# Keeping the sines and cosines of E and the activation hf in PSUM, with two phase buffers and three banks for the gated unit

## The chip, the core and the metric

The kernel runs on one core of one Trainium2 chip. Five engines work side by side there: TensorE (PE, with its weight loads shown apart as PEld), VectorE (DVE), ScalarE (ACT), GpSimd (POOL) and SyncE (SP), the last of which only issues transfers here. Each engine carries out its own list of instructions in order, and instructions on different engines wait for each other through semaphores. TensorE writes its results to PSUM, which this kernel uses as eight banks of 128 partitions by 512 fp32 values; VectorE and ScalarE read and write both PSUM and the large on-chip memory SBUF, and GpSimd works on SBUF alone in this kernel. The metric is the device time of one launch in microseconds (us).

## The reference, cut to what matters

The input `x` has 2048 tokens of 448 channels. After a layer norm the result is the sum of the input, a state-space convolution and a gated unit:

```python
def _A_ref(u, log_A_real, A_imag, C_real, C_imag, log_dt, D_skip):
    L = u.shape[1]
    dt = jnp.exp(log_dt)
    A = -jnp.exp(log_A_real) + 1j * A_imag
    C = (C_real + 1j * C_imag) * dt[:, None]
    pos = jnp.arange(L)
    P = jnp.exp((A * dt[:, None])[:, :, None] * pos[None, None, :])
    K = 2.0 * jnp.einsum("dn,dnl->dl", C, P).real
    ...                                  # y = causal convolution of u with K, by FFT of length 2L
    return y + u * D_skip[None, None, :]

def _B_ref(x, w_gate, w_up, w_down):
    g = jnp.einsum("bsd,df->bsf", x, w_gate)
    u = jnp.einsum("bsd,df->bsf", x, w_up)
    return jnp.einsum("bsf,fd->bsd", _sigmoid(g) * u, w_down)

xn = _layernorm(x)
return x + _A_ref(xn, ...) + _B_ref(xn, ...)
```

There are 448 channels with 256 complex modes each in the convolution, and 1792 hidden columns in the gated unit. All is fp32.

## The kernel before, in words

Two Python generators write the program: `conv()` for the convolution and `glu()` for the gated unit. Each yields after a piece of work with a weight, and the loop at the end of `s4d_glu_kernel` always continues the one whose share of its planned total is smaller, so that pieces of both alternate in the program. A scheduler then sets the order of the instructions on each engine from a simulated timeline: the earlier instruction in the program has precedence, `hp(HP)` lifts instructions ahead of it by 300 places, and `tc.issue_after(ins)` keeps instructions behind another of the same engine. On the chip that order is fixed.

**The convolution** has four stages. The first (to about 130 us of the span) normalises the input, turns it for the gated unit (`x_transpose`), takes the first step of its Fourier transform (`x_spec`, through the PSUM tile `tr`) and prepares the modes' rates, phases and weights (`prep`, `turn`), mostly on VectorE. The second, `kgen` (139 to 541 us), builds the convolution's kernel. Its 56 chunks (`cn`) hold 8 channels each. The exponential of a mode at a position is a product of a factor E, at 64 fine positions, and a factor F, at 32 coarse positions. For each chunk `ahead(cn)` makes the phases of E and F with two matmuls into `tr` (two banks, one buffer), and ScalarE turns them into sines and cosines in the SBUF tile `S` (L547 to L550; two tiles `S0` and `S1` take turns). GpSimd multiplies up the magnitudes `me` and `mf` for two chunks at a time (`magnitudes`, L505 and L517), with two squarings on ScalarE (L530). VectorE multiplies magnitudes with sines and cosines: L604 and L605 make `Et`, L606 makes `Ft`. TensorE sums over the modes, 64 small matmuls a chunk into `ko` (L620). Every four chunks `first_stage` takes a Fourier step of the finished part, through two PSUM tiles `kp` and `kq`, copied to SBUF at L571. `ahead(cn + 1)` stands before the products of `cn` in the program. The third and fourth stages (`spectra`, from about 541 us) multiply the spectra and go back to time.

**The gated unit** goes through two halves of the tokens, and in each through groups of two or three blocks of 128 hidden columns. A step, `gate()`, is one block for 512 tokens: 11 matmuls make the gate's PSUM tile and 11 more the up tile (L712, each operand being split into a high and a low part), ScalarE takes a tanh of the gate into `th` (L720), VectorE makes `hf = (th + 1) * up` (L723), ScalarE rounds it to `hh` (L728), and VectorE takes the rest `hl = hf - hh` (L730). `hf`, `hh` and `hl` are SBUF tiles before the change, so that the bank of the up tile is free once L723 has read it. After a group come eight tiles `po` of the down projection (L826), each added to the accumulator by VectorE at L831. Towards the end of the first half `pair_first` and `pair_turn` bring in the rest of the tokens, through four and two PSUM tiles.

**PSUM before:** the pool `psg` has one tag `gu` with four banks, which the gate and up tiles, `po`, `kq` and the tiles of `pair_first` and `pair_turn` share. The pool `psk` of the first two stages has the other four: `tr` with two, `ko` and `kp` with one each. A tile is given a bank that is free, and its first writer waits for the last reader of the tile that held the bank.

## Time and profile before

| | |
|---|---|
| median of three runs | 728.39 us (727.42 to 731.0) |
| span of the profiled execution, first to last instruction | 723.7 us |
| the profiled execution's own time | not given apart from its span |
| mean granted TensorE clock over the span | 0.983 |
| busy: PE, DVE, ACT, POOL | 676.0, 567.5, 420.8, 380.5 us |
| HBM traffic | 158 GB/s over the span |

The profile comes from one execution. Its span leaves out what lies before the first and after the last instruction; against the median that is 728.39 - 723.7 = 4.7 us. Busy time is the time in which an engine has an instruction under way; matmuls are pipelined, so a busy PE may still wait a little between two of them. A row of a group gives the line, the engine, the operation, the tiles written and read, the shapes, the count, the busy time together and the mean of one in ns, and then the idle time of the engine just before them, with what ended it.

### The profile page before, as it was taken

How to read it: one execution, taken by the hardware profiler on the slowest of the kernel's cores; microseconds unless marked ns; L12 is line 12 of the kernel's file. 1: busy time of each engine (PE TensorE's matmuls, PEld its weight loads, DVE VectorE, ACT ScalarE, POOL GpSimd, SP SyncE). 2: the span in 40 equal slices, each digit the busy share in tenths (PEclk: the TensorE clock that was granted, in tenths of full speed). 3: DMA queues.
4: the chain of work that ended last, by engine and by line, in shares of the span. 5: the costliest groups of instructions: out<-in, count | busy, mean ns of one | idle time of the engine just before them, and what ended most of it. 6: DMA issues, size and time to landing. Idle time of an engine off the chain costs nothing.

```text
span 723.7 us, 19120 instructions
## 1 busy us (share of the span) xinstructions
PE 676.0 (93%) x7789; PEld 532.0 (74%) x7789; DVE 567.5 (78%) x778; ACT 420.8 (58%) x650; POOL 380.5 (53%) x425
## 2 busy tenths in 40 slices
PE   2898799997998999998999999999999999999996
PEld 1675688786876788565777887888877777767785
DVE  5799997699999999999589988987874555655544
ACT  3645455678677778899387777866742222322320
POOL 2120028699888778879646874785864000451002
PEclk9998899999999999999999999999999999999999
DMA  9946328534414445354753242232169999999745
GB/s 204 224 119 186 97 81 251 173 97 167 162 52 135 160 149 173 93 196 141 242 166 120 70 141 87 98 107 72 47 163 247 279 256 218 246 258 244 178 135 163
DMA packets 92711, 115.72 MB, mean 160 GB/s; under 512 B 12432, under 2 KB 81040, under 8 KB 92368
## 3 DMA queue, kind: packets, MB, share of 16 engines
q1 hardware_dynamic: 83040, 93.92, 47.4%
q10 hardware_dynamic: 7040, 14.91, 6.5%
q0 software_dynamic: 2544, 5.67, 3.2%
q8 instruction: 61, 1.00, 0.6%
q14 instruction: 26, 0.21, 0.1%
HBM read 69.70 MB, written 44.76 MB: 158 GB/s over the span
## 4 chain that ended last, share of the span: by engine, by line
PE 69%; DVE 13%; DMA 6%; ACT 5%; issue 3%; SPq 1%; POOL 1%; ACTq 0%; DVEq 0%; POOLq 0%
PE gu L712 28%; PE po L826 16%; PE sp L912 7%; PE ko L620 6%; PE pv L939 4%; PE tr L539 4%; DVE Ft L606 2%; DVE Et L604 2%; DVE Et L605 2%; DMA acc_d<-acc 1%; DVE hl L730 1%; DMA xe<-in_A_u_dram 1%; PE pv L976 1%; PE kp L565 1%; DVE m L321 1%
## 5 line engine op out<-in xcount | busy, mean ns | idle before, releaser
L517 POOL TENSOR_TENSOR me<-me,pm 128x32 f32<-128x32 f32 (+1 forms) x168 | 145.7, 867 | 85.0 <-DVE Et L605 72.9
L517 POOL TENSOR_TENSOR mf<-mf,pm 128x64 f32<-128x64 f32 (+1 forms) x112 | 120.7, 1078 | 4.9
L712 PE MATMUL gu<-xh,wh 128*128 128x512 f32 x336 | 100.3, 404 | 3.2 <-ACT xh L220 3.2
L712 PE MATMUL gu<-xh,wl 128*128 128x512 f32 x336 | 95.9, 393 | 0.0
L712 PE MATMUL gu<-xl,wh 128*128 128x512 f32 x336 | 95.1, 390 | 0.0
L826 PE MATMUL po<-dh,hh 128*128 128x448 f32 (+1 forms) x227 | 86.4, 380 | 6.1 <-DVE acc L831 2.5
L604 DVE TENSOR_TENSOR Et<-me,S 128x1024 f32<-128x1024 f32 x56 | 82.3, 1470 | 8.8 <-ACT S L550 4.5
L605 DVE TENSOR_TENSOR Et<-me,S 128x1024 f32<-128x1024 f32 x56 | 79.0, 1411 | 8.5 <-ACT me L530 7.6
L606 DVE TENSOR_TENSOR Ft<-mf,S 128x1024 f32<-128x1024 f32 x56 | 79.9, 1426 | 6.8 <-ACT S L550 4.4
L826 PE MATMUL po<-dl,hh 128*128 128x448 f32 (+1 forms) x227 | 84.2, 371 | 0.0
L826 PE MATMUL po<-dh,hl 128*128 128x448 f32 (+1 forms) x227 | 83.5, 369 | 0.0
L547 ACT ACTIVATE S<-tr 128x1024 f32<-128x1024 f32 x56 | 57.8, 1032 | 41.0 <-PE tr L539 33.4
L712 PEld LDWEIGHTS gu<-xh,wh 128*128 128x128 f32 x336 | 61.3, 190 | 22.3 <-ACT xh L220 4.6
L728 ACT CAST hh<-hf 128x512 fp32r<-128x512 f32 x56 | 35.0, 625 | 71.1 <-DVE hf L723 59.8
L712 PEld LDWEIGHTS gu<-xh,wl 128*128 128x128 f32 x336 | 63.3, 189 | 15.0 <-DVE pl L313 0.7
L620 PEld LDWEIGHTS ko<-Et,Ft 128*32 128x32 f32 x3584 | 53.5, 110 | 27.4 <-issue 17.1
L712 PEld LDWEIGHTS gu<-xl,wh 128*128 128x128 f32 x336 | 63.0, 188 | 14.0 <-issue 0.7
L620 PE MATMUL ko<-Et,Ft 128*32 128x64 f32 x3584 | 63.6, 222 | 9.2 <-DVE Ft L606 4.7
L723 DVE SCALAR_TENSOR_TENSOR hf<-th,gu 128x512 f32<-128x512 f32 x56 | 38.1, 680 | 37.4 <-PE gu L712 27.7
L550 ACT ACTIVATE S<-S,hpi 128x1024 f32<-128x1024 f32 x56 | 65.5, 1170 | 0.0
L831 DVE SCALAR_TENSOR_TENSOR acc<-po,acc 128x448 f32<-128x448 f32 (+1 forms) x81 | 48.7, 610 | 19.4 <-PE po L826 19.3
L730 DVE TENSOR_TENSOR hl<-hf,hh 128x512 fp32r<-128x512 f32 x56 | 51.2, 914 | 12.6 <-ACT hh L728 12.6
(199 smaller groups left out, 1288.6 us busy)
## 6 DMA issues: line engine op xcount, KB each, us to landing
sk_d<-sk ACTq DMA_DIRECT2D x14, 512.0 KB
sx<-x_d SPq DMA_DIRECT2D x32, 224.0 KB
skl<-sk_d SPq DMA_DIRECT2D x16, 448.0 KB
vp<-v_d SPq DMA_DIRECT2D x16, 448.0 KB
v_d<-vt SPq DMA_DIRECT2D x60, 112.0 KB
wt_d<-wh SPq DMA_DIRECT2D x9, 512.0 KB
wt_d<-wl SPq DMA_DIRECT2D x9, 512.0 KB
wl<-wt_d SPq DMA_DIRECT2D x9, 512.0 KB
```

The lines of the kernel that those rows point to most:

```text
L517: ins = nc.gpsimd.tensor_tensor(m[:, :, w + a : 2 * w : n], m[:, :, a:w:n], par(base + i).unsqueeze(2).to_broadcast([128, 4 * DC, w // n]) ...
L547: nc.scalar.activation(rows(cs), pv, AF.Abs)
L550: sins[:] = [nc.scalar.activation(cs, cs, AF.Sin, scale=-TWO_PI, bias=hpi)]
L604: v.tensor_tensor(Et[:, :, :, 32:64], two(me[:, :, 32:64]), S[:, 1::-1], ALU.mult)
L605: v.tensor_tensor(Et[:, :, :, 0:32], two(me[:, :, 0:32]), S[:, 1:3, :, ::-1], ALU.mult)
L606: fts[:] = [v.tensor_tensor(Ft, two(mf), S[:, 3:5], ALU.mult)]
L620: nc.tensor.matmul(ko[32 * j : 32 * j + 32, sl], Ft[:, cc, DC * h + 4 * q + j], Et[:, cc, DC * h + 4 * q + j], start=(k == 0), stop=(k == ...
L712: glu_mm[:] = [nc.tensor.matmul(ps, a_, b_, start=(n == 0), stop=(n == len(mm) - 1))]
L730: v.tensor_tensor(hl, hf, hh, ALU.subtract)
L826: glu_mm[:] = [nc.tensor.matmul(po[:, ds], a_[:, bs], w_[:, ds], start=(n == 0), stop=(n == 3 * fc - 1))]
L831: v.scalar_tensor_tensor(acc[:, b, ds], po[:, ds], 0.5, acc[:, b, ds], ALU.mult, ALU.add)
L912: mm = nc.tensor.matmul(to, tb[:kk, t, 64 * c : 64 * c + 64], rhs, start=True, stop=True, skip_group_check=True,)
```

## The change

The tile `tr` gets two buffers of two banks. Each of its two banks now holds one kind of phase, E's or F's, in place of half of the modes of both; so `ahead` needs four matmuls of 256 columns where it had two of 512, with each block of phases loaded as weights twice. ScalarE takes the absolute values of both into `S` (one instruction, as before), and then four instructions of 512 elements make the sine of F in `S`, the sine of E in its own place in PSUM, the cosine of E in the bank that held F's phases, and the cosine of F in `S`. The negated sine of E is no longer made. `S` shrinks from five parts to three.

VectorE reads the sines and cosines of E from PSUM. The product for the upper 32 positions stays one instruction of 1024 elements; that for the lower 32 becomes two of 512, the second of which (`scalar_tensor_tensor`) also changes the sign. The product for F reads `S` as before.

In `gate()`, `hf` is no longer a tile of its own: L723 writes it over the up tile in PSUM, and L728 and L730 read it there.

The tag `gu` has three banks instead of four. `ko` keeps its bank; the separate bank of `kp` is gone, and `kp` and `kq` both take banks of `gu`. `x_spec`, `turn` and the first `x_transpose` use the buffers of `tr`.

```diff
         if nb == 4:
-            two = psc[-1].tile([128, 2, 512], F32, name="tr", bufs=1)
-            banks = [two[:, 0], two[:, 1]] + [psc[-1].tile([128, 512], F32, name=n, bufs=1) for n in ("ko", "kp")]
+            two = [psc[-1].tile([128, 2, 512], F32, name="tr", bufs=2) for _ in range(2)]
+            banks = [t[:, i] for t in two for i in range(2)]
...
-                ps = psg.tile([128, 512], F32, name="gu", bufs=4)
+                ps = psg.tile([128, 512], F32, name="gu", bufs=3)
...
-            ("S1", [128, 5, 2 * DC, 32], F32), ("Et1", [128, 2, 2 * DC, 64], F32),
+            ("S1", [128, 3, 2 * DC, 32], F32), ("Et1", [128, 2, 2 * DC, 64], F32),
...
             S = tl[f"S{cn % 2}"]
-            ps = psc[-1].tile([128, 2, 512], F32, name="tr", bufs=1)
+            ps = psc[-1].tile([128, 2, 512], F32, name="tr", bufs=2)
             ph = pht[cn // 2 % 2]
             for h in range(2):
-                nc.tensor.matmul(
-                    ps[:, h], ph[:, cn % 2, 128 * h : 128 * h + 128], sel, start=True, stop=True
-                )
+                for c in range(2):
+                    x = slice(256 * c, 256 * c + 256)
+                    nc.tensor.matmul(
+                        ps[:, c, 256 * h : 256 * h + 256], ph[:, cn % 2, 128 * h : 128 * h + 128], sel[:, x],
+                        start=True, stop=True,
+                    )
...
-            nc.scalar.activation(rows(cs), pv, AF.Abs)
-            nc.scalar.activation(rows(S[:, 0:5:4]), pv, AF.Sin, scale=TWO_PI)
-            nc.scalar.activation(rows(S[:, 2:3]), pv[:, :, 0:1], AF.Sin, scale=-TWO_PI)
-            sins[:] = [nc.scalar.activation(cs, cs, AF.Sin, scale=-TWO_PI, bias=hpi)]
-            return S
+            ph_e, ph_f = ps[:, 0], ps[:, 1]
+            row = lambda i: S[:, i].rearrange("p m s -> p (m s)")
+            nc.scalar.activation(S[:, 0:2].rearrange("p c m s -> p c (m s)"), ps, AF.Abs)
+            nc.scalar.activation(row(2), ph_f, AF.Sin, scale=TWO_PI)
+            nc.scalar.activation(ph_e, ph_e, AF.Sin, scale=TWO_PI)
+            nc.scalar.activation(ph_f, row(0), AF.Sin, scale=-TWO_PI, bias=hpi)
+            sins[:] = [nc.scalar.activation(row(1), row(1), AF.Sin, scale=-TWO_PI, bias=hpi)]
+            return S, ps.rearrange("p c (m s) -> p c m s", s=32)
...
             pss = [
-                psc[-1].tile([128, 8, 2, 32], F32, name="kp", bufs=1),
-                psg.tile([128, 8, 2, 32], F32, name="kq", tag="gu", bufs=4),
+                psg.tile([128, 8, 2, 32], F32, name=n, tag="gu", bufs=3) for n in ("kp", "kq")
             ]
...
-                v.tensor_tensor(Et[:, :, :, 32:64], two(me[:, :, 32:64]), S[:, 1::-1], ALU.mult)
-                v.tensor_tensor(Et[:, :, :, 0:32], two(me[:, :, 0:32]), S[:, 1:3, :, ::-1], ALU.mult)
-                fts[:] = [v.tensor_tensor(Ft, two(mf), S[:, 3:5], ALU.mult)]
+                lo = me[:, :, 0:32]
+                v.tensor_tensor(Et[:, :, :, 32:64], two(me[:, :, 32:64]), ee[:, ::-1], ALU.mult)
+                v.tensor_tensor(Et[:, 0, :, 0:32], lo, ee[:, 1, :, ::-1], ALU.mult)
+                v.scalar_tensor_tensor(Et[:, 1, :, 0:32], ee[:, 0, :, ::-1], -1.0, lo, ALU.mult, ALU.mult)
+                fts[:] = [v.tensor_tensor(Ft, two(mf), S[:, 1:3], ALU.mult)]
...
-        hf = pg.tile([128, 512], F32, name="hf", bufs=1)
+        hf = pgu[1]
```

17 lines of the change are left out of this document (7 added, 10 removed).

## The prediction

> **What bounds the kernel now.** I read the page first: its span, the busy shares and the engines on the chain that ended last.
>
> ```profile
> span 723.7 us, 19120 instructions
> PE 676.0 (93%) x7789; PEld 532.0 (74%) x7789; DVE 567.5 (78%) x778; ACT 420.8 (58%) x650; POOL 380.5 (53%) x425
> PE 69%; DVE 13%; DMA 6%; ACT 5%; issue 3%; SPq 1%; POOL 1%; ACTq 0%; DVEq 0%; POOLq 0%
> ```
>
> TensorE is busy for 93% of the span and holds 69% of the chain. VectorE, whose work the change lightens, can therefore give back only time in which TensorE stands still. Where that is, the busy times by stage tell: one row each for the first and the second half of the building of the convolution's kernel, and for the spectra.
>
> ```profile
> core 0: us, PE busy (x) PEld busy (x) DVE busy (x) ACT busy (x) POOL busy (x), PEclk, DMA share, GB/s
> 140.00:350.00 210.00, 196.44 (x2877) 151.55 (x2876) 199.28 (x206) 167.93 (x253) 175.82 (x177) 0.98 0.43 136
> 350.00:545.00 195.00, 192.79 (x2982) 159.38 (x2981) 157.70 (x161) 137.27 (x197) 132.03 (x151) 1.00 0.39 121
> 545.00:723.70 178.70, 172.45 (x1405) 131.86 (x1403) 98.08 (x190) 44.74 (x85) 36.26 (x47) 1.00 0.90 222
> ```
>
> From 140 to 350 us VectorE is busy for 95% and TensorE idle for 210 - 196.4 = 13.6 us; the granted clock of 0.98 costs about 0.02 x 210 = 4.2 us more. From 350 to 545 TensorE is idle for 2.2 us with VectorE at 81%; after that VectorE is at 55% and no line of the change has much weight. So the prize lies between 140 and 350 us and is at most 13.6 + 4.2 = 17.8 us, with 2.2 behind it. Third, TensorE's own waits between 130 and 545 us (total, times, longest):
>
> ```profile
> PE ko L620 <- DVE Ft L606: 4.7, 7, 1.9
> PE ko L620 <- DVE Et L604: 4.6, 2, 2.9
> PE kp L565 <- ACT ks L633: 2.5, 3, 1.0
> PE po L826 <- DVE xr L224: 2.4, 2, 1.4
> ```
>
> Three of the four longest, 11.7 us, end with VectorE.
>
> **The products and hl on VectorE.** Durations (shortest, median, longest) of the two products for Et, of hf and of hl:
>
> ```profile
> L604 DVE TENSOR_TENSOR Et<-me,S x56: 1207/1328/2115, 139.2 to 531.3; 128x1024 f32<-128x1024 f32 x56
> L605 DVE TENSOR_TENSOR Et<-me,S x56: 1206/1224/2178, 140.3 to 532.5; 128x1024 f32<-128x1024 f32 x56
> L723 DVE SCALAR_TENSOR_TENSOR hf<-th,gu x56: 627/678/689, 27.9 to 691.8; 128x512 f32<-128x512 f32 x56
> L730 DVE TENSOR_TENSOR hl<-hf,hh x56: 618/691/2645, 30.3 to 693.2; 128x512 fp32r<-128x512 f32 x56
> L419 DVE TENSOR_TENSOR b<-b,m 112x512 f32<-112x512 f32 x2 | 1.4, 680 | 0.0
> ```
>
> L604, L605 and L730 read two SBUF tiles and vary by a factor of 1.8 to 4. L723 has the length of L730 but reads one operand in PSUM, and its 56 instances all lie within 627 to 689 ns, with GpSimd at work beside it for most of the time. I read this as a stretching by GpSimd that a PSUM operand avoids, and price the new instructions at the unstretched lengths: 1207 ns for the 1024 elements of L604, 680 ns for each of the two halves of L605 and for L730. L606 keeps two SBUF operands and its length. The busy time of L604, L605 and L730 in the two stages, in that order:
>
> ```profile
> 140.00:350.00 210.00, 41.46 (x30) 0.98 0.43 136
> 350.00:545.00 195.00, 39.98 (x26) 1.00 0.39 121
> 140.00:350.00 210.00, 44.54 (x30) 0.98 0.43 136
> 350.00:545.00 195.00, 34.46 (x26) 1.00 0.39 121
> 140.00:350.00 210.00, 17.18 (x16) 0.98 0.43 136
> 350.00:545.00 195.00, 16.65 (x18) 1.00 0.39 121
> ```
>
> From 140 to 350 us: L604 41.5 - 30 x 1.207 = 5.3; L605 44.5 - 60 x 0.68 = 3.7; L730 17.2 - 16 x 0.68 = 6.3; together 15.3 us off VectorE's 199.3, which falls to 88%. From 350 to 545 us: 8.6 - 0.9 + 4.4 = 12.1 us, off an engine that was no bound. What reaches TensorE: of the 11.7 us of waits I take 8, as the time won doesn't fall exactly where TensorE waited, and with fewer stops 3 of the 4.2 us of clock: **-11 us**. Bounds: 0, if the waits only move, and -20 (17.8 + 2.2).
>
> [...]
>
> **ScalarE.** The phases' four instructions before:
>
> ```profile
> L547 ACT ACTIVATE S<-tr x56: 1003/1028/1087, 135.1 to 527.8; 128x1024 f32<-128x1024 f32 x56
> L548 ACT ACTIVATE S<-tr x56: 1010/1022/1087, 136.0 to 528.8; 128x1024 f32<-128x1024 f32 x56
> L549 ACT ACTIVATE S<-tr x56: 596/605/667, 136.9 to 529.7; 128x512 f32<-128x512 f32 x56
> L550 ACT ACTIVATE S<-S,hpi x56: 1135/1165/1227, 137.9 to 530.1; 128x1024 f32<-128x1024 f32 x56
> ```
>
> Before 1.03 + 1.02 + 0.61 + 1.17 = 3.82 us. After: the absolute values 1.03, two sines of 512 at 0.61, two cosines with a bias at 1.17 - (1.03 - 0.61) = 0.74 each: 3.72 us. That saves 0.1 us a chunk on an engine at 80%, and E's products may start after four of the five, 0.83 us sooner. I count 0; it widens no wait. A write to PSUM by ScalarE has no row; if it cost as much as an SBUF write, nothing changes.
>
> **TensorE's phases.** Four matmuls of 256 columns instead of two of 512. The end of the trace has matmuls of 448 and 224 columns in a row, the first two rows two apart, the last two eight apart; then the weight load of a phase matmul:
>
> ```profile
> 716.32 0.37 PE L826 MATMUL po<-dh,hh 128*128 128x448 f32 x1
> 716.74 0.37 PE L826 MATMUL po<-dh,hl 128*128 128x448 f32 x1
> 716.94 0.27 PE L826 MATMUL po<-dh,hh 128*128 128x224 f32 x1
> 717.83 0.28 PE L826 MATMUL po<-dh,hl 128*128 128x224 f32 x1
> L539 PEld LDWEIGHTS tr<-sel,ph x112: 186/188/338, 132.0 to 527.2; 128*128 128x128 f32 x112
> ```
>
> Starts are 0.21 us apart at 448 columns and 0.111 us at 224, so about 0.0125 us + 0.44 ns a column: 0.125 us at 256 and 0.24 us at 512. Four against two: 0.50 - 0.48 = +0.02 us, and I take 0.04 us x 56 = **+2.2 us**, since all of it lies on the busy engine. Bounds: 0, and 2 x 0.188 x 56 = +21 us if the two added loads were in the open; in the row of 224 columns they are not. The new second buffer takes no wait in exchange: `tr` of chunk cn + 1 needs the Et products of cn - 1, which the 64 ko matmuls ahead of it needed already.
>
> **Three banks.** An up tile now holds its bank until hl is done. One case (the last matmuls of an up tile, its hf and hl; kp's first matmul, the next gate tile, the copy of kp):
>
> ```profile
> 163.11 0.61 PE L712 MATMUL gu<-xl,wh 128*128 128x512 f32 x2
> 168.27 0.68 DVE L723 SCALAR_TENSOR_TENSOR hf<-th,gu 128x512 f32<-128x512 f32 x1
> 171.98 1.55 DVE L730 TENSOR_TENSOR hl<-hf,hh 128x512 fp32r<-128x512 f32 x1
> 171.60 0.27 PE L565 MATMUL kp<-wk,ks 64*64 64x64 f32 x1 [0.97 <-ACT ks L633]
> 172.69 0.73 PE L712 MATMUL gu<-xh,wh 128*128 128x512 f32 x2
> 178.13 0.61 ACT L571 COPY sk<-kp 128x512 f32<-128x512 f32 x1
> ```
>
> The bank was held for 5.2 us after the last matmul and would be for 9.8. At 172.69 kp, kq, this up tile and the one after it would hold four banks of three; the gate's first matmul, and all ko, tr and po matmuls queued behind it on TensorE, would wait. How often: from 350 to 545 us there are 18 steps and 26 chunks, so 2 + 1.33 (eight po in six steps) + 0.72 (kp and kq every four chunks) = 4.05 tiles a step of 10.8 us, one each 2.7 us; with three banks a bank is wanted again after 8.0 us. An up tile needs about 2.5 us for its matmuls, so hl may end 5.5 us behind them; the case above is 4 us too late. But it comes from the stage in which VectorE is behind, which is what the change eases, and TensorE stopped soon afterwards anyway. I take one step in ten of the 34, at 1 us: **+3 us**. Bounds: 0, and every fourth step at the 4 us of the case, +34.
>
> **Before 140 us.** VectorE has the preparation, without GpSimd, and gains nothing; two buffers spare x_spec a wait, and three banks keep the gated unit from running ahead:
>
> ```profile
> PE tr L285 <- ACT x1ab L296: 4.3, 3, 2.2
> 60.00:80.00 20.00, 13.41 (x64) 8.32 (x61) 19.75 (x31) 13.58 (x19) 0.20 (x1) 0.78 0.60 166
> ```
>
> Bounds -4.3 and +6.6 (that stretch's idle time once more); **+1 us**.
>
> **Sum.** -11 + 2.2 + 3 + 1 = -4.8: span 718.9 us, with the 4.7 us around it **723.5 us**, 0.7% below the median of 728.4; the likeliest case's own range is 718 to 728.
>
> **Rivals.** (1) The banks decide, slower: at TensorE's next gu tile, in-order waits for hl. It decides once one step in six loses 2.5 us, 34 / 6 x 2.5 = 14 instead of 3: 734.5 us. For it: the 9.8 us above against 5.5. Against it: hl itself and the products queued ahead of it get shorter. (2) The relief is mostly hidden: the waits for L604 and L606 are the chunk's chain from ScalarE, not VectorE's queue. Then -4 instead of -11, and with fewer crowded steps +1 for the banks: -4 + 2.2 + 1 + 1 = +0.2, 728.6 us. For it: nine waits only make up the 9.3 us on ko. (3) The whole idle time goes: -20 + 2.2 + 0 + 1, 711.6 us. For it: GpSimd's stretched products get shorter as well. (4) Bank waits break TensorE's stream so often that its clock drops. The rows show 0.98 where it idled for 13.6 us and 1.00 where it idled for 2.2. At 0.97 over both stages 0.03 x 405 = 12.2 us are lost instead of 4.2, and the 3 us of clock are not won: 723.5 + 11 = 734.5 us. [...] (5) The change doesn't do what it says, operands in PSUM being stretched as well: 0 + 2.2 + 3 + 1, 734.6 us; L723 speaks against it.
>
> **How the numbers follow.** Forecast 0.42, (1) 0.18, (2) 0.20, (3) 0.12, (4) 0.05, (5) 0.03. A measurement of this kernel tells about 0.5%, 3.6 us, from no change: below 724.8 is faster, above 732.0 slower. Faster: three quarters of the forecast's 0.42, (3) and a little of (2), 0.46; slower: (1), (4), (5), 0.27 with (2)'s edge; the same 0.27. From (3) to beyond (1) the range is 711 to 736 us.
>
> **What would show it.** Right: the new L604 at 1.2 us throughout, the halves and L730 at 0.68, VectorE near 88% from 140 to 350 us and TensorE's idle time there under 6 us, few waits of gu matmuls for L730. Wrong: gu, po or kp on TensorE waiting for L730 or L571 for over 8 us in total (1), a clock under 0.98 (4), phase matmuls 0.2 us apart, or a product in PSUM beyond 1.4 us (5).

## The result and the profile after

The changed kernel takes 747.95 us (median of 4 runs, 744.63 to 749.59) beside 729.02 us for the kernel before in the same sitting: 1.0256 times as long, with a 95% interval of 1.0210 to 1.0302. The forecast was 723.5 us, with a range of 711 to 736. It is wrong in sign and outside the range.

The lines below come from the changed kernel. Lines of the program have moved: the phase matmuls are L541, E's sines and cosines L551 and L552, Et's products L607 to L609, Ft's product L610, `ko` L624, `kp` L567, the gate's matmuls L716, the tanh L724, `hf` L727, `hl` L734, `po` L830, pair_first's copies L699. First the page: span, busy time, the engines of the chain that ended last.

```profile
span 747.8 us, 19445 instructions
PE 694.3 (93%) x7901; PEld 547.9 (73%) x7901; DVE 529.1 (71%) x834; ACT 406.4 (54%) x706; POOL 283.2 (38%) x425
PE 55%; DVE 15%; DMA 11%; ACT 7%; issue 5%; SPq 3%; POOL 3%; ACTq 1%; DVEq 0%; POOLq 0%
```

VectorE lost 38 us of work and GpSimd 97 us, and yet the span grew by 24.1 us between the two executions profiled; the medians lie 18.9 us apart. TensorE's share of the chain fell from 69% to 55%: more of the time, TensorE was waiting for others. TensorE's idle time grew from 723.7 - 676.0 = 47.7 to 747.8 - 694.3 = 53.5 us. The durations are as priced (shortest, median, longest):

```profile
L607 DVE TENSOR_TENSOR Et<-me,tr x56: 1205/1214/1222, 137.3 to 544.8; 128x1024 f32<-128x1024 f32 x56
L608 DVE TENSOR_TENSOR Et<-me,tr x56: 672/680/683, 138.4 to 545.9; 128x512 f32<-128x512 f32 x56
L609 DVE SCALAR_TENSOR_TENSOR Et<-tr,me x56: 675/684/689, 139.0 to 546.5; 128x512 f32<-128x512 f32 x56
...
L734 DVE TENSOR_TENSOR hl<-gu,hh x56: 632/688/693, 30.1 to 716.2; 128x512 fp32r<-128x512 f32 x56
...
L610 DVE TENSOR_TENSOR Ft<-mf,S x56: 1209/1226/2152, 134.4 to 552.0; 128x1024 f32<-128x1024 f32 x56
```

L607, L608, L609 and L734, with one operand in PSUM, vary by 10% at most, and the halves, at medians of 680 and 684 ns, last about as long as the prediction's L419 (680 ns), which works on 512 elements in SBUF alone. L610, which still reads two SBUF tiles, reaches 2152 ns. So the change does on VectorE what it says. The stages tell where the time went. First the changed kernel (columns as in the prediction: PE, PEld, DVE, ACT, POOL, then the granted clock), then the kernel before for the windows that the prediction doesn't show:

```profile
140.00:350.00 210.00, 195.47 (x2883) 153.39 (x2881) 165.90 (x220) 154.45 (x268) 109.99 (x164) 0.96 0.41 128
350.00:560.00 210.00, 201.45 (x3026) 167.49 (x3024) 146.98 (x196) 131.23 (x225) 99.27 (x152) 0.98 0.37 117
...
0.00:140.00 140.00, 119.27 (x550) 91.72 (x551) 116.02 (x230) 74.75 (x125) 35.59 (x61) 0.98 0.66 172
140.00:300.00 160.00, 150.32 (x2343) 124.69 (x2342) 135.17 (x176) 120.44 (x205) 93.05 (x137) 0.99 0.40 132
300.00:360.00 60.00, 53.68 (x586) 35.14 (x585) 36.48 (x54) 37.94 (x72) 20.56 (x37) 0.86 0.48 136
```

```profile
0.00:140.00 140.00, 114.32 (x531) 89.23 (x532) 112.47 (x222) 70.90 (x116) 36.44 (x52) 0.95 0.65 170
140.00:300.00 160.00, 151.14 (x2238) 122.04 (x2240) 153.01 (x152) 126.32 (x184) 135.78 (x134) 0.98 0.40 132
300.00:360.00 60.00, 55.30 (x816) 37.58 (x805) 49.85 (x60) 46.31 (x76) 48.39 (x57) 0.97 0.59 177
```

As an estimate, I add up what TensorE loses in a window: its idle time, and the window's length times what the granted clock lacks to 1. From 300 to 360 us this is 4.7 + 0.03 x 60 = 6.5 us before and 6.3 + 0.14 x 60 = 14.7 us after. From 140 to 300 us it is 8.9 + 3.2 = 12.1 before and 9.7 + 1.6 = 11.3 after: this stretch, in which most of the 11 us was to be won, wins 0.8. From 350 to 560 us it is 8.5 + 4.2 = 12.7 after, where before (350 to 545 us in the prediction) 2.2 us were idle. Until 140 us TensorE is busy for 5 us more than before. The windows don't hold the same work in both kernels, so the sums show the place and not the last microsecond.

TensorE's waits in the changed kernel (total, times, longest), and then six of them in order of time, with the idle time and its end in brackets:

```profile
...
PE tr L541 <- DVE Et L609: 5.8, 3, 3.7
PE kp L567 <- ACT ks L637: 3.7, 2, 3.0
...
PE gu L285 <- ACT x L699: 2.5, 4, 0.9
...
PE ko L624 <- DVE Ft L610: 1.7, 2, 1.1
...
PE gu L716 <- DVE hl L734: 1.1, 1, 1.1
```

```profile
305.72 2.64 PE L285 MATMUL gu<-xt,wx 32*64 32x448 f32 x8 [1.90 <-DVE xr L224]
322.10 0.97 PE L285 MATMUL gu<-xt,wx 32*64 32x448 f32 x4 [0.90 <-ACT th L724]
323.78 1.76 PE L285 MATMUL gu<-xt,wx 32*64 32x448 f32 x8 [0.71 <-ACT x L699]
337.46 0.97 PE L285 MATMUL gu<-xt,wx 32*64 32x448 f32 x4 [0.95 <-ACT x L699]
...
353.80 0.74 PE L830 MATMUL po<-dh,hh 128*128 128x448 f32 x1 [0.87 <-ACT x L699]
...
527.17 0.63 PE L541 MATMUL tr<-sel,ph 128*128 128x256 f32 x4
531.51 0.98 PE L541 MATMUL tr<-sel,ph 128*128 128x256 f32 x3 [3.71 <-DVE Et L609]
```

`ko` hardly waits for VectorE any more: 1.7 us instead of 9.3. In exchange the phase matmuls wait for the Et products that still hold their two banks, most of all at 531 us. From 300 to 360 us, where the gated unit brings in the second half of the tokens (called the turn stage below), all waits shown are for a bank: pair_first's matmuls (L285) need one that a copy (L699), a tanh (L724) or pair_turn's last subtraction (L224) has yet to leave, and one `po` does.

Points at which TensorE has done the same matmuls in both profiles show more than windows of the same time. At the last matmul of pair_first, 1792 of the 3584 `ko` matmuls, 616 of the 1232 for gate and up tiles and 312 of the 681 records of `po` are done in both kernels; at the last `ko` matmul, 1012 and 528 of the latter two. The first row of each pair is the turn stage, here from the first to the last matmul of pair_first, and the second goes on to the last `ko` matmul. First the kernel before:

```profile
296.80:344.90 48.10, 43.81 (x680) 27.48 (x681) 44.46 (x52) 43.88 (x74) 40.72 (x43) 0.96 0.51 156
344.90:538.90 194.00, 191.08 (x2915) 157.94 (x2915) 160.07 (x167) 135.57 (x194) 130.90 (x152) 1.00 0.39 121
```

Then the changed kernel:

```profile
302.80:352.90 50.10, 44.65 (x488) 27.44 (x488) 33.37 (x48) 33.31 (x64) 14.22 (x24) 0.86 0.46 133
352.90:558.40 205.50, 198.23 (x2967) 165.94 (x2965) 143.53 (x191) 128.13 (x221) 97.76 (x151) 0.98 0.37 115
```

Where the turn stage begins, the changed kernel is 6.0 us later but three chunks further (1536 `ko` matmuls against 1344), which is about 5 us of TensorE's work (1.1 us for a chunk's `ko` matmuls and 0.6 us for its phases in this trace): it is about level with the kernel before, and on balance nothing is won. At the end of the stage it is 8.0 us behind, at the last `ko` matmul 19.5 and at the end 24.1. So in these two executions a third of the loss is made by the end of the turn stage and two thirds behind it. Of the latter, one piece is the wait of 3.71 us at 531 us with the low clock around it. From 520 to 540 us the changed kernel loses 3.7 + 3.4 = 7.1 us (first row), the kernel before 0.7 (second row):

```profile
520.00:540.00 20.00, 16.29 (x205) 13.92 (x202) 12.81 (x16) 13.24 (x23) 8.62 (x11) 0.83 0.45 128
520.00:540.00 20.00, 19.32 (x330) 15.86 (x332) 15.91 (x17) 10.72 (x16) 10.44 (x13) 1.00 0.61 160
```

### The profile page after: what moved, and what is told of

Its sections match the earlier page's. It is cut to its first block, busy times and chain, and to the rows that moved or that the text cites. A ratio compares the mean times of both kernels' runs of the same rounds, so it can differ in the third digit from the quotient of the medians.

```text
span 747.8 us, 19445 instructions
## 1 busy us (share of the span) xinstructions
PE 694.3 (93%) x7901; PEld 547.9 (73%) x7901; DVE 529.1 (71%) x834; ACT 406.4 (54%) x706; POOL 283.2 (38%) x425
## 4 chain that ended last, share of the span: by engine, by line
PE 55%; DVE 15%; DMA 11%; ACT 7%; issue 5%; SPq 3%; POOL 3%; ACTq 1%; DVEq 0%; POOLq 0%
PE gu L716 23%; PE po L830 13%; PE sp L916 5%; PE ko L624 5%; PE tr L541 3%; PE pv L943 3%; DVE Ft L610 2%; DMA acc<-in_A_u_dram 1%; DMA vp<-v_d 1%; DMA wraw<-in_B_w_gate_dram 1%; POOL me L517 1%; ACT S L549 1%; SPq L652 1%; DMA acc_d<-acc 1%; DMA xe<-in_A_u_dram 1%
## 5 line engine op out<-in xcount | busy, mean ns | idle before, releaser
L517 POOL TENSOR_TENSOR me<-me,pm 128x32 f32<-128x32 f32 (+1 forms) x168 | 115.6, 688 | 166.9 <-DVE Et L609 151.4
L716 PE MATMUL gu<-xh,wh 128*128 128x512 f32 x336 | 104.8, 419 | 2.8 <-DVE hl L734 1.1
L716 PE MATMUL gu<-xh,wl 128*128 128x512 f32 x336 | 97.8, 399 | 0.0
L716 PE MATMUL gu<-xl,wh 128*128 128x512 f32 x336 | 96.4, 393 | 0.0
L830 PE MATMUL po<-dh,hh 128*128 128x448 f32 (+1 forms) x227 | 88.4, 389 | 5.7 <-ACT th L724 2.6
L610 DVE TENSOR_TENSOR Ft<-mf,S 128x1024 f32<-128x1024 f32 x56 | 77.7, 1387 | 20.0 <-PE ko L624 16.9
L830 PE MATMUL po<-dl,hh 128*128 128x448 f32 (+1 forms) x227 | 85.1, 375 | 0.0
L830 PE MATMUL po<-dh,hl 128*128 128x448 f32 (+1 forms) x227 | 85.0, 374 | 0.0
L607 DVE TENSOR_TENSOR Et<-me,tr 128x1024 f32<-128x1024 f32 x56 | 68.0, 1214 | 15.9 <-ACT tr L552 14.3
L716 PEld LDWEIGHTS gu<-xh,wh 128*128 128x128 f32 x336 | 60.2, 194 | 23.2 <-issue 4.4
L716 PEld LDWEIGHTS gu<-xh,wl 128*128 128x128 f32 x336 | 64.3, 192 | 15.0 <-issue 0.7
L517 POOL TENSOR_TENSOR mf<-mf,pm 128x64 f32<-128x64 f32 (+1 forms) x112 | 72.5, 647 | 7.1
L732 ACT CAST hh<-gu 128x512 fp32r<-128x512 f32 x56 | 33.1, 591 | 76.1 <-DVE gu L727 63.8
L727 DVE SCALAR_TENSOR_TENSOR gu<-th,gu 128x512 f32<-128x512 f32 x56 | 38.6, 690 | 50.6 <-PE gu L716 34.3
L716 PEld LDWEIGHTS gu<-xl,wh 128*128 128x128 f32 x336 | 63.6, 190 | 14.4 <-issue 0.7
L624 PEld LDWEIGHTS ko<-Et,Ft 128*32 128x32 f32 x3584 | 54.0, 111 | 19.9 <-issue 15.3
L624 PE MATMUL ko<-Et,Ft 128*32 128x64 f32 x3584 | 64.6, 223 | 1.7 <-DVE Ft L610 1.7
L724 ACT ACTIVATE th<-gu 128x512 f32<-128x512 f32 x56 | 33.8, 604 | 49.6 <-PE gu L716 49.6
L734 DVE TENSOR_TENSOR hl<-gu,hh 128x512 fp32r<-128x512 f32 x56 | 38.4, 685 | 30.2 <-ACT hh L732 30.2
L830 PEld LDWEIGHTS po<-dh,hh 128*128 128x128 f32 x227 | 44.3, 195 | 17.0 <-issue 3.5
```

Source lines behind the costliest of these rows:

```text
L517: ins = nc.gpsimd.tensor_tensor(m[:, :, w + a : 2 * w : n], m[:, :, a:w:n], par(base + i).unsqueeze(2).to_broadcast([128, 4 * DC, w // n]) ...
L607: v.tensor_tensor(Et[:, :, :, 32:64], two(me[:, :, 32:64]), ee[:, ::-1], ALU.mult)
L610: fts[:] = [v.tensor_tensor(Ft, two(mf), S[:, 1:3], ALU.mult)]
L624: nc.tensor.matmul(ko[32 * j : 32 * j + 32, sl], Ft[:, cc, DC * h + 4 * q + j], Et[:, cc, DC * h + 4 * q + j], start=(k == 0), stop=(k == ...
L716: glu_mm[:] = [nc.tensor.matmul(ps, a_, b_, start=(n == 0), stop=(n == len(mm) - 1))]
L724: marks[0] = nc.scalar.activation(th, pgu[0], AF.Tanh, scale=0.5)
```

## The experiments

The changes in us below are ratios taken times 728 us. In all of them but one (the relief alone) the scheduler makes TensorE's order anew, so I begin with the parts of the change and then ask what such a reordering costs by itself.

**hf alone**, the kernel before with `hf` written over the up tile:

```diff
-        hf = pg.tile([128, 512], F32, name="hf", bufs=1)
+        hf = pgu[1]
```

> The kernel before with one edit: hf is written over the up tile in PSUM; four banks for gu, phases and sines as before. Theory A (the loss comes from gu having three banks instead of four, with four tiles or more wanting them): four banks cover the longer hold of the up tile, hl falls from a mean of 914 to about 690 ns, 724 to 729 us. Theory B (what hurts is that an up tile holds its bank until hl is done, whatever the number of banks): 735 us or more, with gu or po matmuls waiting for hl. Theory C (the loss comes from the sines and cosines of E in PSUM, whose phase tile waits for ScalarE and VectorE): as A, 724 to 729 us.

734.15 us, ratio 1.0068 (1.0043 to 1.0092). This lies between the forecasts of A and B. With four banks it gains nothing, though `hl`'s longest instance falls from 2645 to 693 ns.

**The bank cut alone**, the kernel before with three banks and one left unused:

```diff
-                psg.tile([128, 8, 2, 32], F32, name="kq", tag="gu", bufs=4),
+                psg.tile([128, 8, 2, 32], F32, name="kq", tag="gu", bufs=3),
...
-        pss = [psg.tile([128, 512], F32, name="gu", bufs=4) for _ in range(4)]
+        pss = [psg.tile([128, 512], F32, name="gu", bufs=3) for _ in range(4)]
...
-            ps = psg.tile([128, 512], F32, name="gu", bufs=4)
+            ps = psg.tile([128, 512], F32, name="gu", bufs=3)
...
-                            po = psg.tile([128, D], F32, name="po", tag="gu", bufs=4)
+                            po = psg.tile([128, D], F32, name="po", tag="gu", bufs=3)
```

> The kernel before with one edit: gu has three banks instead of four; one bank of the eight stays unused, kp keeps its own, hf and the sines stay in SBUF. Theory A: the cut of the bank alone costs 10 to 20 us, 738 to 748 us, most of it from 300 to 360 us of the span, where pair_first asks for four tiles at once. Theory B: without the longer hold three banks are enough, 728 to 732 us. Theory C: 728 to 732 us.

743.35 us, ratio 1.0203 (1.0140 to 1.0267), or +14.8 us: by far the largest part of the loss, with not one operand moved.

```profile
140.00:300.00 160.00, 149.08 (x2249) 121.13 (x2247) 155.61 (x154) 126.17 (x182) 139.50 (x132) 1.00 0.42 134
300.00:360.00 60.00, 52.13 (x564) 32.13 (x565) 38.26 (x49) 41.91 (x69) 28.99 (x39) 0.86 0.45 130
```

In the turn stage TensorE loses 7.9 + 8.4 = 16.3 us here, 9.8 more than before; from 140 to 300 us it loses 10.9, not more than the 12.1 before.

**The changed kernel with hf back in SBUF:**

```diff
-        hf = pgu[1]
+        hf = pg.tile([128, 512], F32, name="hf", bufs=1)
```

> The changed kernel with hf back in SBUF; three banks, two buffers of phases and the sines of E in PSUM stay. Theory A: the shortage at pair_first and at kp and kq stays, 742 to 750 us. Theory B: the up tile's bank is free after hf, 725 to 733 us. Theory C: 745 to 750 us.

740.94 us, ratio 1.0172 (1.0117 to 1.0226). The bank cut together with E in PSUM costs about as much as the bank cut alone: E's relief brings at most a few us. The rest, 0.8%, goes with `hf` in PSUM, about as with four banks; what follows shows how little a difference of this size says.

**One phase buffer and four banks**, the changed kernel otherwise (the other tiles of the two tags follow):

```diff
-            ps = psc[-1].tile([128, 2, 512], F32, name="tr", bufs=2)
+            ps = psc[-1].tile([128, 2, 512], F32, name="tr", bufs=1)
...
-                psg.tile([128, 8, 2, 32], F32, name=n, tag="gu", bufs=3) for n in ("kp", "kq")
+                psc[-1].tile([128, 8, 2, 32], F32, name="kp", bufs=1),
+                psg.tile([128, 8, 2, 32], F32, name="kq", tag="gu", bufs=4),
...
-            ps = psg.tile([128, 512], F32, name="gu", bufs=3)
+            ps = psg.tile([128, 512], F32, name="gu", bufs=4)
```

> The changed kernel with four banks for gu again and kp in its own bank, paid for by one buffer of phases instead of two; sines and cosines of E and hf stay in PSUM. The next chunk's phases must then wait for this chunk's products. Theory A: the loss goes as far as the single phase buffer lets it, 722 to 735 us, with TensorE's phase matmuls waiting for the Et products. Theory B: 740 us or more. Theory C: worse than the changed kernel, 750 us or more.

841.0 us, ratio 1.1527 (1.1464 to 1.1590).

```profile
140.00:300.00 160.00, 132.98 (x1797) 109.59 (x1796) 102.90 (x143) 94.38 (x156) 68.82 (x109) 0.88 0.34 110
```

With the sines in PSUM a phase tile lives until the products have read it, and with one buffer TensorE, in order, stands for 27 us of these 160. So E in PSUM, in this form, needs the two banks that the gated unit and `kp` gave up.

**Two reorderings of the kernel before**, by one weight that decides how the pieces of the two generators alternate, 14.2 in the first and 15 in the second; instructions and banks are the same:

```diff
-        yield 14
+        yield 14.2
```

> The kernel before with one planner weight changed: kgen's first yield, after its opening loads, gives 14.2 in place of 14. No instruction is added, removed or resized and all tiles keep their banks; only the order in which the scheduler puts the pieces of the two generators changes, on TensorE in the middle of the program. Theory A (three banks are too few, a shortage of a resource): 728 to 731 us, no change, as nothing gets scarcer. Rival D (the order of before is a lucky one and any reshuffling of it costs 0.5 to 2%, whatever was changed): 733 to 742 us. If D, part of what the bank cut and hf alone cost is reshuffling.

> The kernel before with the same planner weight at 15 in place of 14, a second and larger reshuffling with the same instructions and the same banks. Theory A (shortage of banks): 726 to 732 us. Rival D (any reshuffling costs): 733 to 745 us, like the bank cut alone (743).

727.62 us, ratio 1.0010 (0.9977 to 1.0043), and 734.13 us, ratio 1.0068 (1.0029 to 1.0106). So a reordering alone may cost 5 us, as much as `hf` alone. That `hf` in PSUM slows the kernel by itself is therefore not shown; that it doesn't speed it up is. The bank cut's 2% lies beyond both, but not beyond a third reordering, of the turn stage (below, 2.45%), so its size alone doesn't show that a bank was missed.

**Where the fourth bank is missed.** First, pair_first alone gets the unused bank of the second experiment; then, in the changed kernel, the pieces between the two tiles of a gate step go ahead of both:

```diff
-        pss = [psg.tile([128, 512], F32, name="gu", bufs=3) for _ in range(4)]
+        pss = [psg.tile([128, 512], F32, name=n, bufs=c) for n, c in (("pf", 1),) + 3 * (("gu", 3),)]
```

> The kernel before with three banks for the gated unit (743.35 us alone), but the first of pair_first's four tiles gets the unused fourth bank, so pair_first has as many banks as before and all else has three. Theory A1 (the shortage bites where pair_first takes four tiles while a gate tile is held, 300 to 360 us, where the granted clock is 0.86): 730 to 734 us, clock there 0.95 or more. Theory A2 (the shortage is everywhere in the gated unit): 741 to 745 us. Rival D (reshuffling): anywhere from 730 to 745 us, and the clock from 300 to 360 us doesn't follow the bank.

740.15 us, ratio 1.0175 (1.0139 to 1.0211), the clock from 300 to 360 us still at 0.86.

```diff
         pgu = []
+        if between:
+            between()
         for i in range(2):
...
                 yield 2.5
-                if between:
-                    between()
```

> The changed kernel with the work between the two tiles of a gate step (pair_norm, pair_first) moved ahead of the step's first tile, so that no gate tile is held while pair_first takes its four banks. Theory A1: the granted clock from 300 to 360 us rises from 0.86 to 0.95 or more and the time falls from 748 to 735 to 740 us. Theory A2: 744 to 748 us, the clock there stays under 0.9. Rival D: anywhere from 735 to 750 us, without the clock there following.

747.77 us, ratio 1.0284 (1.0234 to 1.0335), the clock there at 0.83. Both speak against A1: not pair_first's four tiles alone, and not the gate tile held beside them.

**The cover of that stage.** In the kernel before, the turn stage runs beside 816 matmul records in 60 us, in the changed one beside 586, and most of the difference is `ko` (544 records against 324). I took this for the cause and changed the weight of the stage, so that more or less of the convolution stands beside it (6 in three kernels, 0 in the kernel before with less cover):

```diff
                     if cross:
-                        yield 2
+                        yield 6
```

> The changed kernel with one planner weight raised: the pieces of the stage in which the gated unit brings in the rest of the tokens (about 300 to 360 us, pair_norm, pair_turn, pair_first) count 6 instead of 2, so the program puts more of the convolution's chunks beside them (between the first and the second pair of pair_first four chunks, as in the kernel before; the changed kernel has two). Theory F (the loss falls there because the three-bank order leaves TensorE without convolution to fill the waits of that stage): 735 to 741 us in place of 748, granted clock from 300 to 360 us 0.95 or more. Theory A2 (bank waits everywhere, whatever the cover): 744 to 750 us, clock there under 0.9.

> The bank cut alone (743.35 us) with the same weight at 6. Theory F: 730 to 736 us, clock from 300 to 360 us 0.95 or more. Theory A2: 741 to 746 us.

> The kernel before, four banks and all, with the same weight at 0 in place of 2: two chunks of the convolution in place of four between the first and the second pair of pair_first. Theory F: 734 to 742 us and a clock from 300 to 360 us of 0.92 or less, without any bank taken away. Theory A2: 726 to 731 us.

> hf in PSUM alone, four banks (734.15 us), with the same weight at 6. Its convolution was 7 us ahead at 308 us and 7 us behind at 349 us. Theory F: 724 to 729 us, as the lead is kept. Theory A2 (the cover doesn't matter): 732 to 737 us.

751.39 us, 1.0328 (1.0259 to 1.0396); 741.81 us, 1.0178 (1.0127 to 1.0229); 747.31 us, 1.0245 (1.0191 to 1.0299); 731.27 us, 1.0034 (1.0002 to 1.0066). The stage is sensitive: the kernel before loses 2.45%, more than theory F said, with all its banks when convolution is taken from it.

```profile
300.00:360.00 60.00, 54.72 (x578) 35.83 (x578) 43.33 (x52) 43.15 (x72) 34.78 (x45) 0.86 0.57 162
```

(This is the kernel before with less cover: 5.3 + 8.4 = 13.7 us lost where it was 6.5.) But the cover doesn't bring the three-bank kernels back, although it is there: 798 records in these 60 us in the changed kernel and 735 in that of the bank cut. So theory F explains how the place can hurt and not what the bank cut does there; for the changed kernel it fell. The last of the four runs lies between the two forecasts. Its window is a warning: 4.8 us idle and a clock of 0.86, 13.2 us lost, in a kernel that is slower by 0.34% as a whole. A window's loss alone is no measure of the total.

**A bank held by a dummy tile.** The kernel before keeps its four banks, and one is occupied, by a tile written and read once, around the turn stage (shown; from 276.6 to 370.6 us in the profile) or everywhere but there (held from the start to 287.2 us and from 356.8 us to the end of the gated unit). `ac_ins` is the latest addition to the accumulator:

```diff
...
+    def hold():
+        t = psg.tile([128, 512], F32, name="held", tag="gu", bufs=4)
+        with tc.issue_after(ac_ins[0].ins) if ac_ins else nullcontext():
+            v.tensor_copy(t[:, 0:1], one)
+        held_bank.append(t)
...
+    def let_go():
+        with tc.issue_after(ac_ins[0].ins):
+            v.tensor_copy(junk, held_bank.pop()[:, 0:1])
...
                 if cross:
+                    hold()
...
+                if cross:
+                    let_go()
```

> The kernel before with one of its four banks held by a dummy tile (written once, read once) only while the gated unit brings in the rest of the tokens (about 290 to 360 us); four banks elsewhere. TensorE's order is that of before up to there and that of three banks from there on. Theory G (the three banks cost their 14 us in that stage alone): 738 to 744 us, clock from 300 to 360 us 0.90 or less. Theory A2 (they cost it everywhere): 728 to 733 us.

> The complement: a dummy tile holds one of the four banks from the start to that stage and from its end to the end of the gated unit, and the stage itself has four. Theory G: 727 to 733 us, clock from 300 to 360 us 0.95 or more. Theory A2: 738 to 744 us.

746.45 us, ratio 1.0257 (1.0202 to 1.0313), and 733.24 us, ratio 1.0088 (1.0054 to 1.0122). First the bank held around the stage, then its complement:

```profile
300.00:360.00 60.00, 53.46 (x607) 33.16 (x607) 42.82 (x47) 40.10 (x66) 34.70 (x38) 0.74 0.39 107
```

```profile
300.00:360.00 60.00, 54.49 (x720) 36.46 (x717) 46.21 (x57) 45.07 (x76) 38.85 (x44) 0.97 0.53 157
```

Both times lie just above theory G's ranges and far from A2's: G holds for the kernel before. The 94 us with one bank less cost 18.7 us (14.7 to 22.8), with 6.5 + 15.6 = 22.1 us of TensorE's time lost in the window. The other 663 us with one bank less cost 6.4 us (3.9 to 8.9), hardly more than the reordering with weight 15. The two don't add up to the 14.8 us of the whole cut, and need not, as each has an order of its own.

Between the same two matmuls of pair_first as above, the stage with the bank held, with four banks (the complement), and in the changed kernel with `hf` in SBUF, which has three:

```profile
299.90:361.60 61.70, 54.55 (x612) 33.45 (x611) 44.52 (x50) 41.74 (x69) 34.80 (x38) 0.75 0.41 114
304.10:348.90 44.80, 40.70 (x548) 25.24 (x547) 35.66 (x45) 36.02 (x62) 30.33 (x34) 0.96 0.50 149
301.90:358.80 56.90, 51.40 (x556) 32.49 (x555) 33.45 (x48) 35.17 (x67) 17.36 (x29) 0.79 0.41 117
```

With the bank held the stage takes 13.6 us longer than the 48.1 us before, with 68 matmul records fewer in it. At about 550 records it takes 44.8 us with four banks and 56.9 with three. With more cover it takes 62.3 us at 743 records after the bank cut, and 57.2 us at 809 records with four banks and `hf` in PSUM. The cover doesn't explain that, and in the kernel with the bank held nearly all the loss is made here: it is 16.7 us behind the kernel before at the end of the stage and 17.8 at the end. What no run separates is how much of it are waits on the chip and how much the order that the scheduler made for the banks it had: TensorE's order with the bank held departs from that of before at 275 us.

**The relief alone.** To see what a faster VectorE is worth when no bank, operand or order on TensorE changes, most of GpSimd's multiplications are taken away (lines not shown set the columns left out to 1):

```diff
...
                         ins = nc.gpsimd.tensor_tensor(
-                            m[:, :, w + a : 2 * w : n],
-                            m[:, :, a:w:n],
-                            par(base + i).unsqueeze(2).to_broadcast([128, 4 * DC, w // n]),
+                            m[:, 0:2, w + a : 2 * w : n],
+                            m[:, 0:2, a:w:n],
+                            par(base + i)[:, 0:2].unsqueeze(2).to_broadcast([128, 2, w // n]),
```

> The kernel before with GpSimd's magnitudes cut to 2 of their 32 channel columns (the rest stays at 1, so this leaves most of the magnitudes out): same instructions, banks and order on TensorE, but GpSimd nearly idle and VectorE's products of two SBUF tiles unstretched, for Et, Ft and hl alike. My prediction's step (relief of VectorE reaches TensorE as 11 us, up to 20 with the stretching gone from Ft too): 708 to 718 us. Rival H (the relief is hidden, TensorE's time doesn't hang on it): 724 to 730 us.

716.22 us, ratio 0.9840 (0.9792 to 0.9888), or -11.6 us.

```profile
140.00:300.00 160.00, 157.97 (x2361) 126.44 (x2359) 133.69 (x164) 133.90 (x199) 67.62 (x135) 1.00 0.44 145
300.00:360.00 60.00, 57.09 (x847) 41.56 (x843) 43.34 (x59) 46.72 (x76) 22.30 (x51) 0.97 0.67 196
```

From 140 to 300 us TensorE loses 2.0 us instead of 12.1, with VectorE at 133.7 us of work, nearly what it has in the changed kernel (135.2). TensorE's matmuls come in the same order as before, all 7789, and the first of pair_first comes at 286.0 us instead of 296.8. H fell. VectorE's nearly equal relief in the changed kernel left TensorE's loss there at 11.3 us. The two reliefs are not the same, though: here Ft's product gets shorter too (1.24 us instead of 1.48 on average in this window, 1.45 in the changed kernel), and GpSimd's own busy time in the window falls from 135.8 to 67.6 us (93.1 in the changed kernel).

**The preparation's two buffers alone**, for x_spec, turn and the first x_transpose (one of the three is shown), in a PSUM pool of their own that closes before the chunks:

```diff
-            ps = psc[-1].tile([128, 2, 512], F32, name="tr", bufs=1)
+            ps = psc[-1].tile([128, 2, 512], F32, name="tr", bufs=2)
...
+            with tc.tile_pool(name="psp", bufs=1, space=PSUM) as pp_, tc.tile_pool(
                 name="pst", bufs=1, side="right", reuse_waits="tile"
             ) as pst:
+                psc.append(pp_)
```

> The kernel before with two buffers of tr in the preparation only (a PSUM pool of its own that is closed before the chunks begin); banks of the gated unit and chunks as before. In the changed kernel the first chunk came 7 us sooner. If the preparation's two buffers are what gave it and the lead lasts: 720 to 725 us. If the lead is lost at the stage from 300 to 360 us, as in the other kernels whose convolution came there early: 727 to 735 us.

727.67 us, ratio 1.0006 (0.9982 to 1.0030).

```profile
0.00:140.00 140.00, 121.35 (x621) 93.00 (x622) 119.19 (x230) 76.41 (x124) 38.81 (x61) 0.99 0.65 173
...
300.00:360.00 60.00, 54.56 (x708) 38.18 (x707) 47.35 (x56) 43.22 (x71) 38.63 (x51) 0.89 0.63 184
```

With the two buffers TensorE is busy for 7 us more until 140 us than in the profile of before (5 in the changed kernel). Against the run with the bank held, whose order is that of before until 275 us and which is at 116.0 us, it is 5 us (3). In the run with `hf` alone, without these buffers, it is 119.3 us, so the changed kernel's 119.27 needn't come from them. The turn stage takes the lead back: 5.4 + 6.6 = 12.0 us lost there, 5.5 more than before.

**The turn stage off the three banks.** At last the changed kernel with pair_first and pair_turn in the buffers of `tr`, and the stage's weight at 3; then the same with `hf` in SBUF:

```diff
-        pss = [psg.tile([128, 512], F32, name="gu", bufs=3) for _ in range(4)]
+        two = [psc[-1].tile([128, 2, 512], F32, name="tr", bufs=2) for _ in range(2)]
+        pss = [t[:, i] for t in two for i in range(2)]
...
-                        yield 2
+                        yield 3
```

> The changed kernel with pair_first and pair_turn taking their tiles from the two buffers of tr (two banks each) in place of the three banks, so that in the stage from 300 to 360 us the three banks serve the gate, up and po tiles alone; the planner weight of that stage is 3 instead of 2, so that about as many chunks stand beside it as in the changed kernel. Theory G (that stage's lack of a bank hides the relief): 727 to 737 us in place of 748, clock from 300 to 360 us 0.93 or more; if no other part costs anything, 720. Rival J (the shared phase buffers now stall the chunks there, and the relief stays lost): 740 to 750 us, clock under 0.9.

> The same with hf in SBUF as before the change, so the up tile's bank is free after hf. Theory G, if holding the up tile until hl costs in the rest of the program too: 3 to 8 us below the run with hf in PSUM. If with hf's bank it is the turn stage alone that counts: the same within 2 us. If the shorter hl is worth more than the bank: 2 to 5 us above it.

754.36 us, ratio 1.0367 (1.0285 to 1.0449), and 763.58 us, ratio 1.0499 (1.0433 to 1.0566). The stage's clock is 0.88, and the loss goes on behind it:

```profile
300.00:360.00 60.00, 52.73 (x650) 36.99 (x648) 32.83 (x52) 32.86 (x61) 16.36 (x30) 0.88 0.58 174
360.00:520.00 160.00, 151.86 (x2148) 122.96 (x2149) 111.73 (x149) 108.31 (x187) 77.20 (x125) 0.94 0.30 95
```

Rival J, by more than its range: the tiles of the stage now take the phase buffers from the chunks. With `hf` in SBUF it gets slower by another 9 us, beyond all three forecasts, where the changed kernel got faster by 7 us: what `hf` in PSUM costs hangs on the order around it. Eight banks are shared out either way, and no version with E in PSUM that has enough for both was found.

## Why the prediction was wrong

**The relief, -11 us.** Its mechanism is right: with GpSimd's load off, a VectorE that is as much lighter gives 11.6 us (8.2 to 15.1), and the products have the lengths forecast (medians of 1214, 680, 684 and 688 ns, beside 1207 and 680). That the size agrees is in part luck, as that run also shortens Ft's product and GpSimd's own work. The step that failed is that the relief reaches TensorE when the banks are shared out anew: the changed kernel is only level with the kernel before where the turn stage begins. TensorE's waits for VectorE at `ko` went from 9.3 to 1.7 us over the span, and others came in their place, from 140 to 300 us above all `tr` for Et's products (2.1 us) and `kp` for the copy `ks` (3.0, where `kp` waited 1.8 before). Which of them hid how much isn't isolated. VectorE fell from 95% to 79% busy from 140 to 350 us, further than the 88% forecast, and TensorE's idle time there, to be under 6 us, rose from 13.6 to 210 - 195.5 = 14.5 us.

**"The new second buffer takes no wait in exchange"** is a step that failed. `tr` did wait for Et's products, 5.8 us in three waits with 3.7 us at 531 us, where the tile of two chunks earlier was still being read and 7.1 us were lost in 20 with the low clock. I reasoned from the program's order, in which `ko` comes first; the scheduled order puts the phases ahead of it. The run with one phase buffer shows how hard this wait can bite; how much of the whole loss it makes with two isn't isolated.

**Three banks, +3 us** with bounds of 0 and +34, is a term sized far too small: the cut alone measures +14.8 us (10.2 to 19.4), enough to turn the sign of the sum. I had priced it by one case at 168 us, as an up tile held until `hl` ends. But the cut costs its 2% with `hf` in SBUF and no tile held longer, and in the changed kernel gu matmuls waited for `hl` for 1.1 us in all, `kq` for 0.8, far from the 8 us that were to show rival (1). The diff's lines for pair_first and pair_turn, which ask for four and two banks in a stage where gate, up and `po` tiles want theirs, were in the text of the kernel, and I costed neither. Held for 94 us around that stage, one bank costs 18.7 us. This makes rival (1), the banks decide, right in its kind and too small (734.5 us), with the wrong wait and the wrong place.

**The clock.** Rival (4) had it fall over both stages; it fell in the turn stage, to 0.86, and for a short time at 531 us (0.83 from 520 to 540 us). Over the span it went from 0.983 to 0.976 in the executions profiled, which is within the 0.968 to 0.990 that executions of the kernel before show. That waits for banks bring the clock down was my assumption. The changed kernel has such waits of 0.7 to 1.9 us in that stage, with the clock at 0.86, but the kernel before has waits of 0.3 to 1.6 us there at 0.97, so these runs don't settle it.

**The small terms.** The four phase matmuls show no cost in busy time: L541 has 38.0 us where L539 had 41.4, so +2.2 was too much. ScalarE's five instructions have medians of 1.03, 0.59, 0.61, 0.70 and 0.73 us, 3.66 together (3.72 forecast). Before 140 us, priced as 1 us lost, TensorE gains 3 to 5 us, and the turn stage takes a like lead back in the run with the two buffers alone. The sum itself slipped by 0.1: 718.9 + 4.7 is 723.6. Rival (2) had the relief mostly lost, as it was, but for another reason, which the run with GpSimd's load off speaks against, and its 728.6 us is 19 us short; (3) is out by the sign, (5) by the durations.

**What is open.** That a bank missing around the turn stage costs the kernel before over 2% is shown, with the order that goes with it. In the changed kernel it is not shown to be the main cause. For it speak its bank waits in the stage, the 56.9 us that the stage takes with `hf` back in SBUF, and that more cover didn't help. The like window (0.86, with 14.7 us lost, against 16.3 for the bank cut alone) says little, as the kernel before with less cover has 0.86 and 13.7 us with four banks. Against it as the whole cause speaks that only 8.0 of 24.1 us are lost by the end of the stage; of the rest, only the 7.1 us around 531 us have a place and a wait. The repair tried took the banks from the chunks. `hf`'s 0.7 to 0.8% may be the held bank or the reordering.

## What to carry to other kernels

When a change pays for relief with buffers, price the buffers first, in the stage that asks for the most of them at once, and not only where the change happens: in the kernel before, one bank less for 94 of 728 us, around code that runs only there, cost 2.6%. Before reading a part's cost from its own run, measure what a reordering with nothing else changed costs (here 0.1%, 0.7% and, in the turn stage, 2.45%). Compare two profiles where the same matmuls are done, not only at the same time: that shows where a kernel falls behind. And an operand that moves to PSUM lengthens the life of its bank from the first read to the last (with one phase buffer TensorE stood for 27 of 160 us): list who allocates it next, in the order that the engine really has.

## What was not expected of the hardware

TensorE's granted clock doesn't follow a stage's idle time. From 300 to 360 us the kernel before idles for 4.7 us at 0.97, and `hf` alone with more cover for 4.8 us at 0.86. With the bank held it is 6.5 us at 0.74: 1.8 us more idle time than before go with 13.8 us of clock. What the clock does follow is open.

GpSimd gains from VectorE's PSUM operands as well, though no GpSimd instruction changed. Its two groups of products, after and then before:

```profile
L517 POOL TENSOR_TENSOR me<-me,pm 128x32 f32<-128x32 f32 (+1 forms) x168 | 115.6, 688 | 166.9 <-DVE Et L609 151.4
...
L517 POOL TENSOR_TENSOR mf<-mf,pm 128x64 f32<-128x64 f32 (+1 forms) x112 | 72.5, 647 | 7.1
```

```profile
L517 POOL TENSOR_TENSOR me<-me,pm 128x32 f32<-128x32 f32 (+1 forms) x168 | 145.7, 867 | 85.0 <-DVE Et L605 72.9
L517 POOL TENSOR_TENSOR mf<-mf,pm 128x64 f32<-128x64 f32 (+1 forms) x112 | 120.7, 1078 | 4.9
```

The mean falls from 867 to 688 and from 1078 to 647 ns. In four kernels in which E's sines and cosines and `hf` stay in SBUF (the bank cut alone, the same with pair_first's fourth bank, and the two reorderings) the means are 857 to 895 and 1080 to 1098 ns; in the changed kernel with the pieces ahead of the gate step they are 699 and 631. So the gain goes with the operands moved to PSUM, and not with the bank cut or the order. What slows the two engines beside each other isn't shown.

ScalarE writes PSUM about as fast as SBUF, which the trace of before couldn't show. The durations of the sine of F, written to SBUF (L550), of the sine of E, written to PSUM (L551), and of the cosine of E, written to PSUM (L552):

```profile
L550 ACT ACTIVATE S<-tr x56: 572/594/657, 130.8 to 539.1; 128x512 f32<-128x512 f32 x56
L551 ACT ACTIVATE tr<-tr x56: 582/607/653, 133.6 to 540.2; 128x512 f32<-128x512 f32 x56
L552 ACT ACTIVATE tr<-S,hpi x56: 667/704/760, 136.1 to 540.8; 128x512 f32<-128x512 f32 x56
```

And, from the tile `S`, the cosine of F, which goes to SBUF:

```profile
L553 ACT ACTIVATE S<-S,hpi x56: 712/732/776, 133.0 to 539.5; 128x512 f32<-128x512 f32 x56
```

The sine to PSUM is 13 ns longer than the one to SBUF, and the cosine to PSUM is 28 ns shorter.
